# Spreading a bound over the partitions: a product with ones (sum) in place of a product with the identity and a maximum

## The chip, the cores and the metric

One core of a Trainium2 chip runs the whole program in one launch. The metric is device time in microseconds (us). The kernel before was run three times on its own: 1235.79, 1236.59 and 1240.24 us; the median is 1236.59 us.

## The reference

Three layers follow each other. An attention over 4 batches, 8 heads, 576 positions and head size 64 keeps only scores within tau of their row's maximum. Its output, 2304 tokens by 512, goes through two dense layers with a hidden size of 2048, each with its own elementwise function between two products.

```python
scores = scale * np.matmul(q, k.transpose(0, 1, 3, 2))
thresh = np.max(scores, axis=-1, keepdims=True) - tau
scores = np.where(scores >= thresh, scores, -1000000000.0)
attn = np.exp(scores - np.max(scores, axis=-1, keepdims=True))
attn = attn / (np.sum(attn, axis=-1, keepdims=True) + 1e-09)
x = np.matmul(attn, v)                      # heads side by side: 2304 x 512
...
h = x @ w_in                                # first layer ("moe1")
P = a[0] + a[1] * h + a[2] * h2 + a[3] * h3
Q = 1.0 + np.abs(b[0]) * np.abs(h) + np.abs(b[1]) * h2
x = (P / (Q + 1e-06)) @ w_out
...
h = x @ w_in                                # second layer ("moe2")
g = np.where(h >= 1, h, np.where(h <= -1, 0.0, (h + 1) ** 2 / 4.0))
out = g @ w_out
```

## The kernel before

**Two halves for every number.** TensorE multiplies in float16. Every operand is therefore scaled by a power of two and split into a high and a low half, and a product is three products of halves. The scale must come from a bound on the operand's size, and all 128 partitions must use the same one. So for each piece of input the kernel computes a number in each partition, brings these 128 numbers together in every partition, and then takes a power of two from the result (`root`: a shift and mask at L169, a multiply and maximum at L172, a reciprocal at L173). Bringing them together is the job of `everywhere` (L179): for each of n columns a float32 product of the column, repeated 128 times, with the identity matrix puts all 128 numbers side by side in every partition (L188), and VectorE takes their maximum (L189).

**Where it is called.** Each of the two layers has 8 chunks of weights with 2 halves each: x = 0 from w_in, x = 1 from w_out. `convert` (L233) loads a half (1 MB), turns it from wide words into float32 on VectorE (L229 to L231), lets TensorE build a product of it with itself (L254), reduces that on VectorE (L255) into `bound`, calls `everywhere` and `root`, and splits (`split`: ScalarE L218 and L209, GpSimd L213). `prep_pair` (L334) does the like for q and k of a pair of heads, with two columns (n = 2): squares summed on ScalarE (L345), `everywhere`, `root`, some small constants, then the split (L215, L216) and a transposing DMA of the halves (L365). `everywhere` is also called for v, for the norm of the first layer's weights and for each block of tokens between the two layers (L189 with place = acc).

**The order of work.** The first stage does batch 0's attention in a form of its own (`first_attention`), beside it all 16 halves of moe1's weights, and after that the 16 halves of moe2's weights (`stage_half`). Then come 8 phases, moe1 and moe2 for each batch; a phase is 24 steps: 3 blocks of 192 tokens by 8 chunks. A step is one `first_product` (24 matmuls, L863), the elementwise function on ScalarE, VectorE and GpSimd, and three steps later one `second_product` (24 matmuls, L877). When a chunk has been used for the last time in a phase its place is taken by the other layer's chunk, 1 MB from DRAM (`load_chunk`, L278). Attention of batch b + 1 runs beside the steps of batch b: for each of 4 pairs of heads 9 score rows, each with scores on TensorE (L396, L397), the clamp and row maximum on VectorE (L442), exponential on ScalarE (L403), mask on VectorE (L404), halves on ScalarE and GpSimd, a transposing DMA (L417) and the product with v (L430).

Every piece of code is given a priority by the step at which it is due (`at`), and a scheduler that estimates the engines' times puts all instructions in order on each engine ahead of the run. Each engine, and the DMA queue of SyncE (SP), then runs its list strictly in that order. Any instruction that is removed or gets another length can therefore move others, also far away.

Of the kernel before, what the change touches and what calls it, by code (L numbers as in the profile page):

```python
# [10 lines left out]
F32 = mybir.dt.float32  # L11
# [32 lines left out]
def tile_attention_moe_moe2(  # L44
# [18 lines left out]
    V, A, G, T, Q = nc.vector, nc.scalar, nc.gpsimd, nc.tensor, nc.sync  # L63
    B, H, S, D = q.shape
    P = 128
# [24 lines left out]
    ps_1 = ctx.enter_context(tc.tile_pool(name="ps_1", bufs=1, space=PSUM))  # L90
# [18 lines left out]
    def small(n, name, keep=False):  # L109
        if keep:  # L110
            return cp.tile([P, n], F32, name=name)
        tag = "".join(x for x in name if x.isalpha() or x == "_").rstrip("_")
        return sp.tile([P, n], F32, name=name, tag=f"s{n}_{tag}", bufs=4 if tag in ("mx", "nt") else 2)
# [51 lines left out]
    def root(name, f, src, up, even=False, n=1, keep=False):  # L165


        s = small(n, name + "_s", keep)
        V.tensor_scalar(f.bitcast(I32), src.bitcast(I32), 1, 0x3F000000 if even else 0x3F800000,  # L169
                        op0=ALU.logical_shift_right, op1=ALU.bitwise_and)  # L170
        top = TOP / 2 if even else TOP
        V.tensor_scalar(f, f, up / top, (2.0 if even else 1.0) * TINY / top, op0=ALU.mult, op1=ALU.max)  # L172
        V.reciprocal(s, f)  # L173
        return s
# [5 lines left out]
    def everywhere(name, src, n, keep=False, place=None):  # L180


        r = small(n, name, keep)
        if place is None:
            place = ps_1.tile([P, 512], F32, name="pm" + name, tag="aux")
        pm = place[:, 0 : n * P].rearrange("p (n q) -> p n q", n=n)
        for i in range(n):
            T.matmul(pm[:, i], src[:, i : i + 1].to_broadcast([P, P]), ident, start=True, stop=True)  # L188
        V.tensor_reduce(r, pm, axis=AX.X, op=ALU.max)  # L189
        return r  # L190

    wide = w1_in.dtype != F32
    words = 2 if wide else 1
    raw_type = I32 if wide else F32
# [5 lines left out]
    f_w = [[small(NCH, f"f_w{m}{x}", True) for x in range(2)] for m in range(2)]  # L202
# [3 lines left out]
    def split(hi, lo, src, scale=None, on_vector=True):  # L206

        if scale is None:
            A.copy(hi, src)  # L209

            n = E // 4 if tuple(src.shape) == (P, E) else None
            for p in [slice(c, c + n) for c in range(0, E, n)] if n else [slice(None)]:
                G.tensor_tensor(lo[:, p], src[:, p], hi[:, p], op=ALU.subtract)  # L213
        elif on_vector:
            A.activation(hi, src, AF.Copy, scale=scale)  # L215
            V.scalar_tensor_tensor(lo, src, scale, hi, op0=ALU.mult, op1=ALU.subtract)  # L216
        else:
            A.activation(src, src, AF.Copy, scale=scale)  # L218
            split(hi, lo, src)

    def as_float(raw, name):

        if not wide:
            return raw
        src = raw.rearrange("p (n w) -> p n w", w=2)
        t = mp.tile([P, E], I32, name="wt" + name, tag="wt", bufs=N_WT)
        V.tensor_scalar(t, src[:, :, 1], 0x07FFFFFF, 3, op0=ALU.bitwise_and, op1=ALU.logical_shift_left)  # L229
        V.scalar_tensor_tensor(t, src[:, :, 1], -0x40000000, t, op0=ALU.bitwise_and, op1=ALU.bitwise_or)  # L230
        V.scalar_tensor_tensor(t, src[:, :, 0], 29, t, op0=ALU.logical_shift_right, op1=ALU.bitwise_or)  # L231
        return t.bitcast(F32)

    def convert(m, i, x, dst, on_vector):

        if x == 0:
            raw = rp.tile([P, KT, CF * words], raw_type, name=f"rw{m}_{i}_0", tag="rw")
            src = w_in_dram[m][:, i * CF * words : (i + 1) * CF * words].rearrange("(kt p) f -> p kt f", p=P)
        else:
            raw = rp.tile([P, NF, DM * words], raw_type, name=f"rw{m}_{i}_1", tag="rw")  # L240
            src = w_out_dram[m][i * CF : (i + 1) * CF, :].rearrange("(f p) d -> p f d", p=P)
        (A if m == 0 and i == 0 else Q).dma_start(raw, src)
        name = f"{m}_{i}_{x}"
        src = as_float(raw.rearrange("p a b -> p (a b)"), name)
        hi, lo = dst[:, 0:E], dst[:, E : 2 * E]
        columns = m == 0 and x == 0
        bound = gram[:, i : i + 1] if columns else small(1, "mb" + name)
        pg = ps_1.tile([P, 512], F32, name="pg" + name, tag="aux")
        parts = NF if columns else 1
        top = src.bitcast(BF16).rearrange("p (n c f w) -> p n c f w", c=parts, f=P, w=2)[..., 1]  # L250
        n = top.shape[1]
        for c in range(parts):
            for k in range(n):
                T.matmul(pg[:, c * P : (c + 1) * P], top[:, k, c], top[:, k, c], start=(k == 0), stop=(k == n - 1))  # L254
        V.tensor_reduce(bound, pg[:, 0 : parts * P], axis=AX.X, op=ALU.max)  # L255
        s = root("pw" + name, f_w[m][x][:, i : i + 1], everywhere("mw" + name, bound, 1), 2.0**64, even=m == 1 and x == 1)
        split(hi, lo, src, s, on_vector)
        if i == NCH - 1 and (m, x) != (0, 0):
            f_max[m][x] = small(1, f"f_max{m}{x}", True)
            V.tensor_reduce(f_max[m][x], f_w[m][x], axis=AX.X, op=ALU.max)  # L260
# [26 lines left out]
    def whole(x):  # L287
        return x[..., 0 : NT * P, :].rearrange("h (p t) d -> p h (t d)", t=NT)
# [45 lines left out]
    def prep_pair(b, pr, on_vector=True):  # L334
        raws = rp.tile([P, 2, C + 1, D], F32, name=f"rqk{b}_{pr}", tag="rqk", bufs=1)
        raw = raws[:, :, 0:C, :]
        for x, src in enumerate((q, k)):
            Q.dma_start(raws[:, x].rearrange("p (a c) d -> p a (c d)", a=2)[:, :, 0 : NT * D],
                        whole(src[b, 2 * pr : 2 * pr + 2]))
            for ab in range(2):  # L340
                Q.dma_start(raw[ab * ST : (ab + 1) * ST, x, NT, :], src[b, 2 * pr + ab, NT * P :, :])
        mx = small(2, f"mqk{b}_{pr}")
        qk = ap.tile([P, 2, C, 2 * D], F16, name=f"qk{b}_{pr}", tag="qk", bufs=1)
        for x in range(2):
            A.activation(qk[:, x, :, 0:D], raw[:, x], AF.Square, scale=2.0**-32, accum_out=mx[:, x : x + 1])  # L345
        f = small(2, f"qkf{b}_{pr}")
        s = root(f"qkr{b}_{pr}", f, everywhere(f"mqke{b}_{pr}", mx, 2), 2.0**96, n=2)

        con = sp.tile([P, 4], F32, name=f"con{b}_{pr}", tag="con", bufs=3)
        V.scalar_tensor_tensor(con[:, 0:1], f[:, 0:1], cflag, f[:, 1:2], op0=ALU.mult, op1=ALU.mult)  # L350
        V.tensor_scalar(con[:, 1:2], con[:, 0:1], -1.0, None, op0=ALU.mult)
        V.scalar_tensor_tensor(con[:, 2:3], s[:, 0:1], tau8, s[:, 1:2], op0=ALU.mult, op1=ALU.mult)
        V.tensor_tensor(con[:, 2:3], con[:, 2:3], tlow, op=ALU.min)
        if b == 0:
            V.tensor_scalar(con[:, 3:4], con[:, 2:3], STEEP, -LARGEST, op0=ALU.mult, op1=ALU.max)
        for x in range(2):
            split(qk[:, x, :, 0:D], qk[:, x, :, D : 2 * D], raw[:, x], s[:, x : x + 1], on_vector)
        if b > 0 or pr < 2:
            qkT = ap.tile([P, 2 * C, P], F16, name=f"qkT{b}_{pr}", tag="qkT")
            qT, kT = qkT[:, 0:C], qkT[:, C : 2 * C]  # L360
            kT2 = ap.tile([P, C, P], F16, name=f"kT2{b}_{pr}", tag="kT2")
            if b == 0 and pr == 0:
                turned(qk, qT, kT, kT2)
                return con, qT, kT, kT2
            Q.dma_start_transpose(out=qkT, in_=qk.rearrange("p x c d -> p (x c d)"))  # L365
        else:
            qT, kT, kT2 = (ap.tile([P, C, P], F16, name=f"{x}{b}_{pr}", tag="eT" if pr == 2 else "hl", bufs=N_ROW)
                           for x in ("qT", "kT", "kT2"))
            for x, t in enumerate((qT, kT)):
                Q.dma_start_transpose(out=t, in_=qk[:, x].rearrange("p c d -> p (c d)"))  # L370
        Q.dma_start(kT2[0:D], kT[D : 2 * D])
        Q.dma_start(kT2[D : 2 * D], kT[0:D])
        return con, qT, kT, kT2
# [515 lines left out]
    for n in range(N_FIRST):  # L889
        with at(36 * n / N_FIRST - 40):  # L890
            next(att)
        while halves and len(halves) * N_FIRST > 2 * NCH * (N_FIRST - 1 - n):
            with at(2.4 * (2 * NCH - len(halves)) - 39.5):
                i, x = halves.pop(0)
# [83 lines left out]
```

## Time and profile before

| | |
|---|---|
| median of three runs | 1236.59 us (1235.79 to 1240.24) |
| the profiled execution's own time | 1239.17 us |
| its span | 1237.1 us |
| mean granted TensorE clock | 0.963 |
| busy: TensorE matmul, weight load | 1095.3 us (89%), 988.4 us (80%) |
| busy: VectorE, ScalarE, GpSimd | 979.3 (79%), 839.5 (68%), 542.7 us (44%) |
| chain that ended last | TensorE 40%, VectorE 24%, DMA 11%, GpSimd 9%, issue 9%, ScalarE 6% |

The shares are averages over stages of very different kinds. Up to about 275 us batch 0's attention and the conversion of the weights fill the time; from 275 us the 8 phases follow, at first with the next batch's attention beside them and from 1046 us without. Steps are counted here by their second product: step 0's starts near 275 us, step 8's near 318, step 24's near 396, step 32's near 429 and step 48's near 524.

### The profile page before, as it was taken

To read this page: it belongs to the slowest core of one execution; us is meant where nothing else is said; L and a number is where in the kernel's file an instruction comes from. 1 tells how busy PE (TensorE), PEld (TensorE's weight loads), DVE (VectorE), ACT (ScalarE), POOL (GpSimd) and SP (SyncE) were. 2 spreads that over 40 slices of the span, in tenths; PEclk is the share of its full clock that TensorE was granted. 3 is DMA by queue.
4 is the path that set the end of the run, shared out by engine and by line. 5 is a ranking of instruction groups with operands and counts; after the bars stand their busy time and mean duration, and the time that the engine had idled before them with its cause. 6 is when DMAs were issued, how large, how long until landed. Compare 5 with 4: busy or idle time off the path is not lost.

```text
span 1237.1 us, 31750 instructions
## 1 busy us (share of the span) xinstructions
PE 1095.3 (89%) x12636; PEld 988.4 (80%) x12636; DVE 979.3 (79%) x2362; ACT 839.5 (68%) x1532; POOL 542.7 (44%) x698
## 2 busy tenths in 40 slices
PE   2778788588899999898888998998899999999998
PEld 1445456477888989898778888997888998999997
DVE  8887896999997377799997766899996768896431
ACT  2577777698887377677875766887675667775332
POOL 2445545656666266322564454223563553222221
PEclk9888888899899999999999999999999999999999
DMA  7677576635269158813785639422984467007000
GB/s 220 224 205 252 210 266 238 220 93 137 49 151 249 29 111 185 218 28 90 183 225 95 115 64 250 136 50 68 242 195 71 81 171 221 15 2 261 15 14 27
DMA packets 217845, 175.51 MB, mean 142 GB/s; under 512 B 179680, under 2 KB 190944, under 8 KB 209504
## 3 DMA queue, kind: packets, MB, share of 16 engines
q1 hardware_dynamic: 216464, 171.38, 52.6%
q8 instruction: 99, 1.62, 0.5%
q10 hardware_dynamic: 1232, 2.10, 0.5%
q14 instruction: 50, 0.41, 0.1%
HBM read 106.83 MB, written 21.50 MB: 104 GB/s over the span
## 4 chain that ended last, share of the span: by engine, by line
PE 40%; DVE 24%; DMA 11%; POOL 9%; issue 9%; ACT 6%; SPq 1%; DVEq 0%; ACTq 0%; POOLq 0%
PE acc L877 15%; PE ph L863 15%; DMA eT<-hl 8%; POOL hl L415 3%; PE pv L613 2%; PE pv L430 2%; DVE t L746 2%; POOL wh L213 2%; DVE e L404 2%; DVE t L751 2%; DVE sc L442 2%; POOL gg L213 1%; DVE t L757 1%; DVE t L748 1%; DVE t L747 1%
## 5 line engine op out<-in xcount | busy, mean ns | idle before, releaser
L877 PE MATMUL acc<-gg,wc 128*128 128x192 f16 x4608 | 427.6, 247 | 10.9 <-DVE mye L189 4.9
L863 PEld LDWEIGHTS <-wc 128*128 128x128 f16 x4608 | 388.9, 99 | 24.4 <-issue 16.5
L877 PEld LDWEIGHTS <-wc 128*128 128x128 f16 x4608 | 384.1, 98 | 12.6 <-issue 11.2
L213 POOL TENSOR_TENSOR gg<-t,gg 128x384 f16<-128x384 f32 x192 | 192.9, 1006 | 380.1 <-ACT gg L209 308.0
L863 PE MATMUL ph<-xT,wc 128*128 128x192 f16 x2304 | 218.1, 252 | 13.3 <-DVE t L748 13.2
L863 PE MATMUL ph<-yT,wc 128*128 128x192 f16 x2304 | 213.4, 246 | 3.7 <-DVE t L748 2.5
L415 POOL TENSOR_TENSOR hl<-e,hl 128x256 f16<-128x256 f32 x216 | 160.6, 764 | 0.0
L209 ACT CAST gg<-t 128x384 f16<-128x384 f32 x192 | 96.9, 508 | 75.1 <-DVE t L810 36.8
L809 DVE SCALAR_TENSOR_TENSOR t<-t,c 128x384 f32<-128x384 f32 x96 | 66.2, 690 | 88.9 <-ACT t L808 87.0
L404 DVE SCALAR_TENSOR_TENSOR e<-sc,nt,e 128x576 f32<-128x576 f32 x108 | 97.5, 903 | 28.1 <-ACT e L403 27.9
L413 POOL TENSOR_TENSOR hl<-e,hl 128x64 f16<-128x64 f32 x108 | 42.3, 391 | 147.7 <-ACT hl L412 134.0
L403 ACT ACTIVATE e<-sc,nt,con 128x576 f32<-128x576 f32 x108 | 93.3, 864 | 4.6 <-POOL hl L415 0.2
L808 ACT ACTIVATE t<-ph,c 128x384 f32<-128x384 f32 x96 | 63.9, 667 | 45.6 <-PE ph L863 45.3
L430 PE MATMUL pv<-v,eT 128*128 128x65 f16 (+3 forms) x1680 | 71.4, 195 | 25.2 <-DMA eT<-hl 24.1
L442 DVE TENSOR_SCALAR_CACHE_REDUCE sc<-s 128x576 f32<-128x576 f32 x108 | 80.8, 748 | 15.2 <-PE s L397 14.5
L412 ACT CAST hl<-e 128x576 f16<-128x576 f32 x108 | 72.1, 667 | 28.6 <-DVE e L404 28.0
L430 PEld LDWEIGHTS <-eT 128*128 128x128 f16 (+1 forms) x1680 | 64.0, 101 | 33.9 <-DMA eT<-hl 30.0
L744 ACT ACTIVATE t<-ph,sc 128x384 f32<-128x384 f32 x96 | 55.3, 576 | 50.6 <-PE ph L863 50.4
L213 POOL TENSOR_TENSOR wc<-wt,wc 128x256 f16<-128x256 f32 x64 | 55.1, 894 | 63.8 <-ACT wc L209 63.8
L749 ACT ACTIVATE t<-t,lc 128x384 f32<-128x384 f32 x96 | 67.8, 708 | 15.3 <-DVE t L746 14.9
L213 POOL TENSOR_TENSOR wh<-wt,wh 128x256 f16<-128x256 f32 x64 | 58.9, 950 | 35.8 <-ACT wh L209 35.7
L751 DVE SCALAR_TENSOR_TENSOR t<-t,ka,t 128x384 f32<-128x384 f32 x96 | 67.7, 705 | 8.7 <-ACT t L750 8.3
(238 smaller groups left out, 1910.9 us busy)
## 6 DMA issues: line engine op xcount, KB each, us to landing
wc<-scratch SPq DMA_DIRECT2D x56, 1024.0 KB, 5.9
rw<-in_moe_w_in_dram SPq DMA_DIRECT2D x15, 1024.0 KB, 5.7
rw<-in_moe_w_out_dram SPq DMA_DIRECT2D x15, 1024.0 KB, 5.4
scratch<-wc SPq DMA_DIRECT2D x8, 1024.0 KB, 4.5
scratch<-wh SPq DMA_DIRECT2D x16, 512.0 KB, 3.7
rqk<-in_q_dram SPq DMA_DIRECT2D x16, 256.0 KB, 3.1
rqk<-in_k_dram SPq DMA_DIRECT2D x16, 256.0 KB, 3.1
kT<-qkT SPq DMA_DIRECT2D x26, 144.0 KB, 2.5
```

The lines of the kernel that those rows point to most:

```text
L209: A.copy(hi, src)
L213: G.tensor_tensor(lo[:, p], src[:, p], hi[:, p], op=ALU.subtract)
L403: A.activation(e, s, AF.Exp, bias=nb, scale=con[:, 0:1])
L404: V.scalar_tensor_tensor(e, s, th, e, op0=ALU.is_ge, op1=ALU.mult)
L412: A.copy(hi, e)
L415: G.tensor_tensor(lo_w[:, p], e[:, whole][:, p], hi[:, whole][:, p], op=ALU.subtract)
L430: T.matmul(pv[rows, 0:w], eT[:, c, cols], vv[:, h * NT + x if x < NT else H * NT + h, at : at + w], start=(n == 0), stop=(n == len(blocks) ...
L442: V.tensor_scalar(s, banks[:, 0:S], 1.0, -LARGEST, op0=ALU.mult, op1=ALU.max, accum_out=mx)
L749: A.activation(r, u, AF.Ln, bias=lc[:, 1:2], scale=lc[:, 0:1])
L751: V.scalar_tensor_tensor(s, s, ka[:, 0:1], r, op0=ALU.add, op1=ALU.mult)
L863: last = T.matmul(ph[:, f, :], w[:, wx, kt, f * P : (f + 1) * P], rhs, start=(n == 0), stop=(n == 3 * KT - 1))
L877: T.matmul(dst, w[:, wx, f, d * P : (d + 1) * P], gg[:, gx, f, :], start=(i == 0 and f == 0 and n == 0 and d % 2 == 0), stop=(i == NCH - 1 ...
```

## The change

A new vector `one` holds 1.0 in every partition, and a new function `total` multiplies a 128 by 128 matrix of ones with the n columns themselves, one float32 product with n columns. Its result is the sum over the partitions instead of the maximum, and it stands in every partition already, so no reduction follows: `root` reads the PSUM tile. `convert` uses `total` for all halves but moe2's w_in (m = 1, x = 0): 24 of 32. `prep_pair` uses it for all 16 pairs. The other callers of `everywhere` stay. Bounds become larger where sums replace maxima; the powers of two follow from them, and nothing else in the code is edited.

```diff
+    one = small(1, "one", True)
+    G.memset(one, 1.0)
+
+    def total(name, src, n):
+
+        pm = ps_1.tile([P, 512], F32, name="ps" + name, tag="aux")[:, 0:n]
+        T.matmul(pm, one.to_broadcast([P, P]), src, start=True, stop=True)
+        return pm
...
-        s = root("pw" + name, f_w[m][x][:, i : i + 1], everywhere("mw" + name, bound, 1), 2.0**64, even=m == 1 and x == 1)
+        s = root("pw" + name, f_w[m][x][:, i : i + 1], (everywhere if m == 1 and x == 0 else total)("mw" + name, bound, 1), 2.0**64, even=m == 1 and x == 1)
...
-        s = root(f"qkr{b}_{pr}", f, everywhere(f"mqke{b}_{pr}", mx, 2), 2.0**96, n=2)
+        s = root(f"qkr{b}_{pr}", f, total(f"mqke{b}_{pr}", mx, 2), 2.0**96, n=2)
```

Lines below the new function are 9 higher in the changed kernel (L255 becomes L264, L278 becomes L287, L417 becomes L426, L442 becomes L451, L748 becomes L757).

**One weight half on VectorE, in the first stage.** The kernel before, around the half of chunk 5 from moe1's w_out (mb: its bound; pmmw: the 128 numbers in PSUM; mw: their maximum; f_w, pw: the two results of `root`; mx: batch 0's row maxima):

```order
L255 TENSOR_REDUCE mb_5_1_1395<-pg_5_1_1396 128x1
L544 TENSOR_REDUCE mx_2_985<-sm_11_1066 128x1
L189 TENSOR_REDUCE mw_5_1_1406<-pmmw_5_1_1407 128x1
L169 TENSOR_SCALAR f_w_136<-mw_5_1_1406 128x1
L172 TENSOR_SCALAR f_w_136<-f_w_136 128x1
L544 TENSOR_REDUCE mx_2_985<-sm_12_1085 128x1
L173 RECIPROCAL pw_5_1_s<-f_w_136 128x1
```

The changed kernel at the same place:

```order
L264 TENSOR_REDUCE mb_5_1_1363<-pg_5_1_1364 128x1
L240 SCALAR_TENSOR_TENSOR wt_6_0_1507<-rw_6_0_1505,wt_6_0_1507 128x1024
L173 RECIPROCAL pw_5_0_s<-f_w_137 128x1
L553 TENSOR_REDUCE mx_2_959<-sm_03_987 128x1
L169 TENSOR_SCALAR f_w_138<-psmw_5_1_1374 128x1
L172 TENSOR_SCALAR f_w_138<-f_w_138 128x1
```

The reduction of L189 is gone, L169 reads the PSUM tile psmw, and the order of the neighbours is another.

**SP's queue at the change from moe1 to moe2 of batch 0.** The kernel before, from the first load of a moe2 chunk (wc) on (eT: transposes of batch 1's rows, the first number the pair of heads; qkT_2: transposed q and k of pair 2; rqk: input of pair 3):

```order
L278 DMA wc_0_3774<-scratch_134 128x4096
L417 DMA_TRANSPOSE eT_1_0_1_5094<-hl_1_0_1_5089 128x9x128
L278 DMA wc_1_3872<-scratch_134 128x4096
L365 DMA_TRANSPOSE qkT_2_4665<-qk_2_4643 128x18x128
L278 DMA wc_2_3939<-scratch_134 128x4096
L417 DMA_TRANSPOSE eT_1_0_2_5138<-hl_1_0_2_5133 128x9x128
L278 DMA wc_3_4044<-scratch_134 128x4096
L371 DMA kT_2_4666<-qkT_2_4665 64x1152
L372 DMA kT_2_4666<-qkT_2_4665 64x1152
L417 DMA_TRANSPOSE eT_1_1_0_5307<-hl_1_1_0_5302 128x9x128
L278 DMA wc_4_4111<-scratch_134 128x4096
L417 DMA_TRANSPOSE eT_1_1_1_5353<-hl_1_1_1_5348 128x9x128
```

The changed kernel, from the same load on:

```order
L287 DMA wc_0_3713<-scratch_136 128x4096
L287 DMA wc_1_3811<-scratch_136 128x4096
L287 DMA wc_2_3878<-scratch_136 128x4096
L426 DMA_TRANSPOSE eT_0_2_1_4770<-hl_0_2_1_4765 128x9x128
L287 DMA wc_3_3980<-scratch_136 128x4096
L287 DMA wc_4_4047<-scratch_136 128x4096
...
L287 DMA wc_7_4512<-scratch_136 128x4096
L374 DMA_TRANSPOSE qkT_2_4598<-qk_2_4579 128x18x128
L380 DMA kT_2_4599<-qkT_2_4598 64x1152
L381 DMA kT_2_4599<-qkT_2_4598 64x1152
L426 DMA_TRANSPOSE eT_0_2_2_4818<-hl_0_2_2_4813 128x9x128
L426 DMA_TRANSPOSE eT_1_0_0_4991<-hl_1_0_0_4986 128x9x128
```

In the kernel before the transposes of pair 1's rows stand between the loads; in the changed kernel the last row of pair 0 and all rows of pair 1 stand behind the eighth load, and only one transpose stands among the loads.

**VectorE in the same place.** The kernel before, third block of tokens of moe1 (t_0_2_1: its second step; sc, e: batch 1's rows):

```order
L442 TENSOR_SCALAR sc_1_0_0_5046,mx_1_0_0_5044<-s_1_0_0_5039 128x576
L746 SCALAR_TENSOR_TENSOR t_0_2_1_3481<-t_0_2_1_3481,qc 128x384
L463 RECIPROCAL rd_0_2_4494<-rd_0_2_4494 128x2
L747 TENSOR_TENSOR t_0_2_1_3482<-t_0_2_1_3482,ph_0_2_1_3456 128x384
L444 TENSOR_SCALAR nt_1_0_0_5045<-mx_1_0_0_5044,con_1_3965 128x1
L465 TENSOR_TENSOR xs_0_2_4497<-pv_0_2_4444,rd_0_2_4494 128x128
L751 SCALAR_TENSOR_TENSOR t_0_2_0_3384<-t_0_2_0_3384,ka_1935,t_0_2_0_3383 128x384
```

The changed kernel, the same step:

```order
L755 SCALAR_TENSOR_TENSOR t_0_2_1_3425<-t_0_2_1_3425,qc 128x384
L766 SCALAR_TENSOR_TENSOR t_0_2_0_3329<-t_0_2_0_3329,t_0_2_0_3330 128x384
L756 TENSOR_TENSOR t_0_2_1_3426<-t_0_2_1_3426,ph_0_2_1_3400 128x384
L757 SCALAR_TENSOR_TENSOR t_0_2_1_3426<-t_0_2_1_3426,ka_1893,ph_0_2_1_3400 128x384
L760 SCALAR_TENSOR_TENSOR t_0_2_1_3426<-t_0_2_1_3426,ka_1893,t_0_2_1_3425 128x384
L755 SCALAR_TENSOR_TENSOR t_0_2_2_3525<-t_0_2_2_3525,qc 128x384
```

Batch 1's rows are no longer between the steps here. In the changed kernel three rows of batch 1 stand in the order between the second products of step 8 and step 24, and the pairs' rows are level again with the kernel before at step 33.

## Rows read from the trace of the kernel before

**Rows 1.** Busy time by stretch: start:end, us, each engine, clock, DMA, GB/s

```profile
0.00:275.00 275.00, 200.01 (x1350) 138.47 (x1351) 233.02 (x518) 189.76 (x301) 137.47 (x164) 0.88 0.66 217
318.00:396.00 78.00, 69.16 (x840) 64.19 (x838) 71.49 (x171) 60.78 (x119) 50.92 (x63) 0.96 0.68 170
396.00:434.00 38.00, 38.00 (x506) 37.69 (x504) 16.91 (x54) 15.16 (x29) 10.26 (x12) 1.00 0.15 34
434.00:512.00 78.00, 73.05 (x963) 66.78 (x960) 59.98 (x154) 56.57 (x110) 44.85 (x66) 0.98 0.75 157
524.00:672.00 148.00, 132.93 (x1641) 126.14 (x1639) 138.08 (x351) 110.25 (x211) 60.16 (x74) 0.99 0.56 131
788.00:919.00 131.00, 118.80 (x1441) 111.76 (x1439) 125.37 (x316) 99.63 (x191) 50.76 (x64) 0.99 0.51 123
1046.00:1237.00 191.00, 184.57 (x2214) 183.32 (x2211) 109.97 (x232) 96.37 (x171) 40.53 (x45) 0.99 0.16 57
```

**Rows 2.** Costliest groups, shapes apart: the instructions that the change touches

```profile
L188 PE MATMUL pmmqke<-ident,mqk 128*128 128x128 f32 x64 | 13.0, 318 | 14.9 <-ACT lc L151 7.8 <-ACT qk L345 7.1
L188 PE MATMUL pmmw<-ident,mb 128*128 128x128 f32 x48 | 12.8, 355 | 9.6 <-DVE mb L255 9.4
L189 DVE TENSOR_REDUCE mw<-pmmw 128x1 f32<-128x128 f32 x32 | 9.1, 283 | 6.0 <-PE pmmw L188 6.0
L189 DVE TENSOR_REDUCE mqke<-pmmqke 128x2 f32<-128x256 f32 x16 | 6.6, 414 | 3.6 <-PE pmmqke L188 3.6
```

**Rows 3.** Single instructions: ns min/median/max, first and last start in us

```profile
L189 DVE TENSOR_REDUCE mw<-pmmw x32: 276/282/293, 20.2 to 264.5; 128x1 f32<-128x128 f32 x32
L169 DVE TENSOR_SCALAR f_w<-mw x32: 131/144/154, 21.5 to 265.2; 128x1 int32<-128x1 int32 x32
L169 DVE TENSOR_SCALAR qkf<-mqke x16: 152/167/875, 18.3 to 938.2; 128x2 int32<-128x2 int32 x16
L462 DVE TENSOR_SCALAR rd<-pv x60: 138/150/160, 305.1 to 1041.7; 128x2 f32<-128x2 f32 x48, 128x1 f32<-128x1 f32 x12
```

**Rows 4.** L189 on VectorE up to 275 us: busy us and count

```profile
0.00:275.00 275.00, 11.98 (x40) 0.88 0.66 217
```

**Rows 5.** Timeline of one pair's call in batch 3's attention: start, us

```profile
936.98 0.53 PEld L188 LDWEIGHTS pmmqke<-ident,mqk 128*128 128x128 f32 x4
937.06 0.64 PE L188 MATMUL pmmqke<-ident,mqk 128*128 128x128 f32 x4
937.73 0.42 DVE L189 TENSOR_REDUCE mqke<-pmmqke 128x2 f32<-128x256 f32 x1 [0.65 <-PE pmmqke L188]
```

**Rows 6.** L442 (one pair of instructions per attention row): busy us and count

```profile
318.00:396.00 78.00, 7.69 (x22) 0.96 0.68 170
396.00:434.00 38.00, 0.76 (x2) 1.00 0.15 34
434.00:512.00 78.00, 13.61 (x36) 0.98 0.75 157
```

**Rows 7.** The chain that ended last, 376 to 402 us: start, us, what

```profile
376.50 8.56 DMA eT<-hl
385.07 8.14 DMA rqk<-in_k_dram
395.64 4.12 PE acc L877 x48
399.76 1.98 PE ph L863 x24
```

**Rows 8.** SP's queue: first and last of the eight chunk loads

```profile
355.53 0.36 SPq L278 DMA_DIRECT2D wc<-scratch  x1
389.28 0.53 SPq L278 DMA_DIRECT2D wc<-scratch  x1
```

**Rows 9.** Who waited for whom, TensorE, whole span: us, times, longest us

```profile
PE pv L430 <- DMA eT<-hl: 24.1, 27, 2.2
```

**Rows 10.** The page: chain that ended last, share of the span by engine

```profile
PE 40%; DVE 24%; DMA 11%; POOL 9%; issue 9%; ACT 6%; SPq 1%; DVEq 0%; ACTq 0%; POOLq 0%
```

## Prediction

> **What bounds the kernel now.** I read the busy time by stretch first [rows 1], because the change touches three kinds of stretch and its worth differs in each. From 1046 us on nothing is edited: TensorE is busy 184.6 of 191 us there, and that part stays. Up to 275 us no engine is full, but VectorE is nearest to it: 233.0 of 275 us, 85%, against 200.0 for TensorE and 189.8 for ScalarE. Where attention runs beside moe1 steps VectorE is the fullest engine: 71.5 of 78 us from 318 to 396, 138.1 of 148 from 524 to 672, 125.4 of 131 from 788 to 919, which is 92 to 96%. From 396 to 434 us there is nearly no attention, TensorE is busy for all 38 us and VectorE for 16.9. So work taken from VectorE counts in the first three kinds of stretch and not in the last. The second view is the costliest groups [rows 2], for the price of what goes; the third is the chain of waits around 380 us [rows 7], for what the new order does.
>
> **The change part by part.**
>
> *Reductions removed.* 24 of the 32 reductions for weight halves go, at 283 ns, and all 16 for pairs, at 414 ns [rows 2]. That is 24 x 0.283 = 6.8 us and 16 x 0.414 = 6.6 us, 13.4 us of VectorE. The halves all lie before 264.5 us [rows 3]. Of the 40 instructions of L189 before 275 us [rows 4] 32 are for halves; two for v and one for the norm leave 5 for pairs. So the first stage loses 6.8 + 5 x 0.414 = 8.9 us of VectorE, and the time after it 11 x 0.414 = 4.6 us.
>
> In the first stage VectorE has 42 us of idle time, mostly waits for others, so not all of the 8.9 us shortens the path. The ends are 0 (all becomes waiting) and 8.9. Nothing there is full enough to hold the path alone, and a reduction of 0.28 us stands in a chain that crosses TensorE, VectorE and ScalarE once per half; I take half, 4.5 us.
>
> After 275 us, about 8 of the 11 pairs lie in stretches where VectorE is 92 to 96% busy. There 0.41 us less is close to 0.41 us: 8 x 0.41 = 3.3 us. The other three lie beside a full TensorE. I take 3.0 us, ends 0 and 4.6.
>
> *L169 reads PSUM.* The row for a small instruction of the same kind that reads PSUM is L462, median 150 ns; L169 from SBUF takes 144 ns with one column and 167 with two [rows 3]. So I cost the move at nothing; the ends are 40 times -17 ns and +6 ns, under 1 us either way. [...]
>
> *TensorE.* A pair's call is four weight loads and four matmuls with 128 columns, 0.64 us on TensorE [rows 5]. The order of the changed kernel has one float32 matmul with two columns in their place, which by the pattern of the others is two loads and two matmuls. Half of 0.64 is 0.32 us less per pair. A half's call keeps both of its loads; its matmuls have 1 column instead of 128. No row shows a float32 matmul of 1 column, so its price lies between nothing and the 355 ns of the 128 columns [rows 2]; I take it that the load sets the pace and nothing is won. The pairs' 0.32 us lies in the same places as the reduction, mostly beside VectorE's work, and I don't count it again; beside a full TensorE it is what makes the other three pairs worth something (3 x 0.32 = 1 us, the upper end of the 3.0 above).
>
> The wait that TensorE has for the bound of a half, L188 on L255, 9.4 us [rows 2], stays: the new matmul needs the same number from the same reduction.
>
> *The new order.* This is the largest unknown. In the kernel before 11 rows of batch 1's attention run from 318 to 396 us (22 instructions, two a row) and one from 396 to 434 [rows 6]. In the changed order only 3 stand between the second products of step 8 and step 24, so 8 rows move from the first stretch, where VectorE is 92% busy and TensorE idles for 8.8 us, to the steps 24 to 33, where TensorE had no gap and VectorE was busy for 16.9 of 38 us. What a row costs TensorE I get from 434 to 512 us: 13 steps at 2 x 1.98 us [rows 7] are 51.5 us, TensorE was busy 73.05 [rows 1], and 18 rows ran there [rows 6], so 1.2 us a row. The first stretch then has 69.2 - 9.6 = 59.6 us of TensorE work; dense it would take 60 us, with all of its present idle time 68.4. I take 66, 12 less than 78. The second takes 9.6 us more. Net 2.4 us less; the ends are 8.8 less (all idle time goes) and, if the rows' own chain holds up the later steps, more than before (the last rival).
>
> *The loads.* In the kernel before the transposes stand between eight 1 MB loads from 355.5 to 389.3 us [rows 8], and the chain that ended last goes through one that took 8.56 us and a load that took 8.14 us beside them [rows 7]. With one transpose among the loads this knot goes. I count nothing for it beyond the 2.4 us, since it is the same idle time.
>
> *Sum.* 4.5 + 3.0 + 2.4 = 9.9 us less. The profiled execution took 1239.17 us (span 1237.1 and 2.1 us around it), 2.6 us above the median of the runs. Its time less the sum is 1229.3, the median less the sum 1226.7; I predict the middle, 1228 us.
>
> **The rivals.**
>
> *The saved time was not on the path.* VectorE's 8.9 us in the first stage become waits for the weights' DMA, GpSimd or ScalarE, and the order after it changes nothing. For it: VectorE already idles 15% there, and the chain of the whole span is VectorE's for only 24% [rows 10]. Against it: 92 to 96% in three later stretches. Then only about 3 us are won: 1233 to 1237 us.
>
> *All of it is on the path.* 8.9 + 4.6 + 8.8 = 22.3 us less, 1214 to 1217 us. Against it: it needs every gap of the first stage to close.
>
> *The rows come too late (slower).* In the changed order 9 rows of pair 1 stand between steps 24 and 33, and each must run through TensorE, VectorE, ScalarE, GpSimd and a transpose before its product with v, which stands in TensorE's own strict order in front of moe2's matmuls. Waits of that kind already cost 24.1 us in 27 times, at most 2.2 us each [rows 9]. If each of 11 rows that moved (those of pair 1 and the last two of pair 0) waits 2.2 us, that is 24 us; against the 7.5 us of direct savings it decides from 0.7 us a row on, and with 1.2 us a row the change is 13.2 - 7.5 = 6 us slower, about 1243 us. For it: the same knot of order and strict queues exists already. Against it: VectorE, ScalarE and GpSimd are less than half busy in that stretch [rows 1], so a row gets through sooner than before.
>
> **How the numbers follow.** A change below 0.5%, 6.2 us, can't be told from none here. The forecast, with everything between 1217 and 1230.4 us, gets 0.54, of which the full saving has 0.04; the saving off the path 0.32; the late rows 0.14, of which a little ends within 0.5%. So faster 0.54, same 0.34, slower 0.12. The range runs from the full saving's upper end, 1217, to 1241, where most of the slower case is still in: outside are about 0.05 below and 0.13 above. The likeliest case alone spans 1220 to 1231.
>
> **What would show it.** L189 should count 25 in place of 65 instructions, L169 should stay near 150 ns, and TensorE's new matmul should take a call to about half for pairs. Step 0's second product should start 4 to 5 us before 275 us; step 33's another 3 us earlier still; VectorE in the stretches of batches 2 and 3 about 1.7 us less busy each, and the stretches as much shorter. TensorE should have hardly a gap between steps 8 and 24. The forecast is wrong if step 0 starts where it did, or if TensorE waits more than 24 us in all for transposes, with the new waits in steps 24 to 38.

## The result and the profile after

The changed kernel takes 1250.1 us (median of 15 runs) where the kernel before takes 1237.0 (15 runs beside it): ratio 1.0098, 95% interval 1.0076 to 1.012. It is slower by 1%, or 12 us by the ratio, where 0.7% faster was forecast. Its profiled execution took 1248.73 us with a span of 1246.9, at a mean granted TensorE clock of 0.949 (0.963 before).

Busy time by stretch of the changed kernel, the stretches cut at the starts of the same steps as in [rows 1] where those were right (24, 33, 48). Columns: us, then busy us (and instructions) of TensorE's matmuls, its weight loads, VectorE, ScalarE, GpSimd; granted clock, DMA share, GB/s.

```profile
0.00:275.00 275.00, 185.96 (x1199) 126.68 (x1200) 226.70 (x490) 185.85 (x295) 145.31 (x164) 0.84 0.70 222
318.00:389.00 71.00, 67.55 (x827) 65.63 (x825) 62.98 (x145) 52.65 (x100) 39.40 (x40) 1.00 0.44 134
389.00:443.00 54.00, 45.56 (x591) 42.33 (x589) 31.39 (x91) 31.24 (x61) 23.70 (x38) 0.94 0.47 82
443.00:534.00 91.00, 82.39 (x1143) 75.92 (x1141) 67.00 (x176) 65.34 (x126) 42.79 (x70) 1.00 0.76 168
1056.00:1247.00 191.00, 184.46 (x2212) 183.20 (x2210) 109.92 (x232) 96.32 (x171) 40.59 (x45) 1.00 0.16 56
```

VectorE is relieved: over the whole span it is busy for 970.4 us against 979.3. In the first 275 us TensorE is busy 14 us less than before as well (186.0 against 200.0 us): by then the changed kernel has got less far. From step 24 to step 33, 389 to 443 us, TensorE stands still for 8.4 of 54 us where it was busy for all of 38. Behind step 33 the stretches are as long as before (91 and 191 us against 90 and 191).

What was edited, by line and tile: out<-in, partitions x elements, count, then busy us and mean ns of one, and the idle time ahead. L200 is the product with ones.

```profile
L200 PE MATMUL psmw<-mb,one 128*128 128x1 f32 x32 | 5.9, 254 | 1.7 <-DVE mb L264 1.7
L200 PE MATMUL psmqke<-mqk,one 128*128 128x2 f32 x32 | 5.6, 246 | 12.0 <-ACT qk L354 12.0
L189 DVE TENSOR_REDUCE mw<-pmmw 128x1 f32<-128x128 f32 x8 | 2.3, 286 | 1.5 <-PE pmmw L188 1.5
```

And L169, the first reader of a bound, one instruction at a time (ns min/median/max): from PSUM in the first two rows, from SBUF in the third.

```profile
L169 DVE TENSOR_SCALAR f_w<-psmw x24: 145/150/160, 19.0 to 254.5; 128x1 int32<-128x1 int32 x24
L169 DVE TENSOR_SCALAR qkf<-psmqke x16: 145/152/160, 15.2 to 950.2; 128x2 int32<-128x2 int32 x16
L169 DVE TENSOR_SCALAR f_w<-mw x8: 140/154/157, 147.0 to 243.8; 128x1 int32<-128x1 int32 x8
```

So each edited instruction costs what it was priced at or less. TensorE's waits over the whole span (us, times, longest) are where the two kernels part; the first row answers [rows 9], 24.1 us before:

```profile
PE pv L439 <- DMA eT<-hl: 41.9, 28, 8.0
...
PE s L405 <- DVE sc L451: 10.6, 8, 6.5
```

The second row is TensorE waiting for VectorE to read a score row out of PSUM. In the kernel before it was:

```profile
PE s L396 <- DVE sc L442: 7.2, 11, 1.3
```

The chain that ended last answers [rows 10]: VectorE's share fell from 24 to 15%, and the time did not.

```profile
PE 38%; DVE 15%; DMA 10%; issue 9%; POOL 7%; ACT 7%; SPq 1%; DVEq 0%; POOLq 0%; ACTq 0%
```

A correction to the text ahead of the prediction: the early step times given there are too late. In the kernel before the second product of step 0 starts at 244 us, not 275, and that of step 8 at 305, not 318; steps 24 to 48 are right. So [rows 1] starts its second stretch 13 us behind step 8; from step 8 on it is:

```profile
305.00:396.00 91.00, 82.16 (x1013) 76.94 (x1010) 84.22 (x198) 73.78 (x147) 61.29 (x74) 0.96 0.63 153
```

Starts of second products, in us, counted in the traces of the profiled executions (the other columns are the experiments below). Each column is one execution, up to 3 us off its kernel's median:

| step | before | after | sum, old order | maximum, new order | three repairs | three repairs, 128 columns |
|---|---|---|---|---|---|---|
| 0 | 244 | 259 | 247 | 256 | 255 | 256 |
| 8 | 305 | 317 | 306 | 315 | 315 | 315 |
| 24 | 396 | 389 | 394 | 387 | 386 | 387 |
| 33 | 434 | 443 | 433 | 440 | 432 | 433 |
| 48 | 524 | 534 | 522 | 531 | 526 | 522 |
| 144 | 1046 | 1056 | 1044 | 1052 | 1050 | 1040 |
| 188 | 1222 | 1232 | 1220 | 1229 | 1227 | 1217 |

The changed kernel is 15 us late at step 0, 12 late at step 8, 7 us early at step 24, 9 late at step 33, and about 10 from there on. From step 8 to step 33 it is 3 us faster than the kernel before (126 us against 129).

### The profile page after: what moved, and what is told of

Its sections match the earlier page's. It is cut to its first block, busy times and chain, and to the rows that moved or that the text cites. A ratio compares the mean times of both kernels' runs of the same rounds, so it can differ in the third digit from the quotient of the medians.

```text
span 1246.9 us, 31660 instructions
## 1 busy us (share of the span) xinstructions
PE 1092.0 (88%) x12604; PEld 987.6 (79%) x12604; DVE 970.4 (78%) x2322; ACT 842.7 (68%) x1532; POOL 549.2 (44%) x699
## 3 DMA queue, kind: packets, MB, share of 16 engines
q10 hardware_dynamic: 1232, 2.10, 0.5%
## 4 chain that ended last, share of the span: by engine, by line
PE 38%; DVE 15%; DMA 10%; issue 9%; POOL 7%; ACT 7%; SPq 1%; DVEq 0%; POOLq 0%; ACTq 0%
PE ph L872 16%; PE acc L886 16%; DMA eT<-hl 6%; POOL hl L424 3%; PE pv L439 2%; DMA qkT<-qk 2%; POOL wh L222 2%; DVE e L413 2%; POOL gg L222 1%; DVE t L760 1%; DVE t L755 1%; DVE t L766 1%; DVE t L756 1%; PE s L405 1%; ACT hl L421 1%
## 5 line engine op out<-in xcount | busy, mean ns | idle before, releaser
L222 POOL TENSOR_TENSOR gg<-t,gg 128x384 f16<-128x384 f32 x192 | 190.0, 991 | 389.1 <-ACT gg L218 310.6
L872 PE MATMUL ph<-xT,wc 128*128 128x192 f16 x2304 | 221.8, 255 | 16.2 <-DVE t L757 7.8
L872 PE MATMUL ph<-yT,wc 128*128 128x192 f16 x2304 | 218.9, 248 | 2.0 <-DVE t L757 2.0
L439 PE MATMUL pv<-v,eT 128*128 128x65 f16 (+3 forms) x1680 | 71.6, 197 | 42.1 <-DMA eT<-hl 41.9
L451 DVE TENSOR_SCALAR_CACHE_REDUCE sc<-s 128x576 f32<-128x576 f32 x108 | 80.8, 749 | 9.6 <-PE s L406 9.0
L222 POOL TENSOR_TENSOR wc<-wt,wc 128x256 f16<-128x256 f32 x64 | 60.7, 980 | 58.2 <-ACT wc L218 58.2
L222 POOL TENSOR_TENSOR wh<-wt,wh 128x256 f16<-128x256 f32 x64 | 63.4, 1019 | 43.9 <-ACT wh L218 43.9
```

The source lines that it names most:

```text
L439: T.matmul(pv[rows, 0:w], eT[:, c, cols], vv[:, h * NT + x if x < NT else H * NT + h, at : at + w], start=(n == 0), stop=(n == len(blocks) ...
L451: V.tensor_scalar(s, banks[:, 0:S], 1.0, -LARGEST, op0=ALU.mult, op1=ALU.max, accum_out=mx)
L872: last = T.matmul(ph[:, f, :], w[:, wx, kt, f * P : (f + 1) * P], rhs, start=(n == 0), stop=(n == 3 * KT - 1))
```

## Experiments

My theory: the new order of the queues is what costs, not the sum. Its first rival: the sum itself (product with ones, PSUM read) costs. Its second: the order of the kernel before is a good draw and any edit loses it. For most of the experiments the order of each engine's queue is written out as a table of positions and chained with issue-order edges (`NoSync`: order without a semaphore). In the traces the sum in the old order and the maximum in the new order run every engine's and SP's sequence of the other kernel, apart from the instructions exchanged.

```diff
+def keep_order(tc):
...
+        for d in steps:
+            at += d
+            x = rows[engine][at]
+            if last is not None:
+                tc.add_manual_dep(x, last.name, mybir.DependencyInfo(mybir.DependencyClass.NoSync, mybir.DependencyReason.DATA), reason="order")
+            last = x
...
     while pending:
         with at(st + 1.5):
             finish_step()
+    keep_order(tc)
```

**Order against sum.** Sum in the old order:

> The changed kernel's instructions, every engine's queue put in the order of the kernel before (the 16 second products and 40 reductions that the change removes are left out of it, the memset of the ones is put in). If the loss is the new order of the queues: 1223 to 1238 us, 12 to 27 below the changed kernel, not above the kernel before. If the sum itself (the product with ones, the read of PSUM) costs: 1245 to 1255, as the changed kernel.

1238.77 us, ratio 1.0026 (1.0009 to 1.0044).

Maximum in the new order:

> The kernel before with its identity products and maxima, every engine's queue put in the order of the changed kernel (the removed instructions stand where their readers stand). If the loss is the order: 1245 to 1262 us, as the changed kernel or up to 9 more, for the 8.9 us of VectorE that it still has. If the sum itself costs: 1232 to 1240, as the kernel before.

1244.56 us, ratio 1.0075 (1.0047 to 1.0103).

Neither theory takes all. The order alone costs 0.75%, the sum alone 0.26%, and together they are the 0.98% of the change. The first run is just above its range and the second just below: 13.4 us less of VectorE in the old order gave nothing. TensorE's two long waits are there with the maximum in the new order (us, times, longest, from 246 to 434 us), where no sum is:

```profile
PE s L517 <- DVE sc L563: 8.0, 2, 6.8
PE pv L551 <- DMA eT<-hl: 6.4, 3, 5.6
```

With the sum in the old order no such wait in that stretch is longer than 1.2 us.

One row for each of four kernels shows that the end of the first stage follows the order and hardly the sum: the last operation of the division on each of batch 0's four pairs (ns min/median/max, first and last start). Before, then sum in the old order:

```profile
L629 DVE SCALAR_TENSOR_TENSOR x<-x,d x4: 747/1164/1220, 90.1 to 227.2; 128x576 f32<-128x576 f32 x4
```

```profile
L761 DVE SCALAR_TENSOR_TENSOR x<-x,d x4: 750/1166/1221, 91.9 to 229.8; 128x576 f32<-128x576 f32 x4
```

Maximum in the new order, then the changed kernel:

```profile
L750 DVE SCALAR_TENSOR_TENSOR x<-x,d x4: 1109/1220/1447, 91.6 to 234.1; 128x576 f32<-128x576 f32 x4
```

```profile
L638 DVE SCALAR_TENSOR_TENSOR x<-x,d x4: 1107/1221/1718, 90.2 to 234.0; 128x576 f32<-128x576 f32 x4
```

The last pair starts this at 227 to 230 us in the old order and at 234 in the new, with a sum or a maximum.

**Where in the order.** New order up to step 0, old behind:

> The changed kernel's instructions; its own order up to the second product of step 0, the order of the kernel before for all that is left. If the place that costs is the first stage (step 0 15 us late): 1245 to 1255 us. If it is the transpose of 8 us at 394 us, behind pair 2's on SP: 1230 to 1240. If the sum itself costs: 1245 to 1255.

1243.84 us, 1.0067 (1.004 to 1.0094).

Old order up to step 0, new behind:

> The changed kernel's instructions; the order of the kernel before up to the second product of step 0, its own order for all that is left. If the place that costs is the first stage: 1225 to 1240 us. If it is the late transpose at 394 us: 1245 to 1255. If the sum itself costs: 1245 to 1255.

1247.41 us, 1.0107 (1.0075 to 1.0139).

The first lies outside its ranges: it loses 0.4% more than the sum in the old order, so the new order costs something in the first stage. The second has the whole loss of the changed kernel with the old order in the first stage. That need not lie far behind the cut: its step 0 starts at 262 us, 15 later than in the sum in the old order, after two waits of TensorE for VectorE at the joint of the two orders (3.9 and 3.1 us, ending at 252 and 258 us). So neither run places the loss cleanly.

The order of the changed kernel with the old one from step 24 on:

> The changed kernel's instructions; its own order up to the second product of step 24, the order of the kernel before for all behind. It keeps what the new order does up to 390 us (TensorE's wait of 6.5 us at 267 us for the first row of batch 1, step 0 15 us later) and loses the late transpose at 394 us. If the late transpose is the greater part: 1240 to 1245 us. If what stands ahead of step 0 is: 1246 to 1252.

1257.35 us, 1.0172 (1.0135 to 1.0209), outside both ranges. The joint itself costs: steps 22 to 24 take 36 us (375 to 411) where the changed kernel takes 12, and nine score rows run there against one; rows that the new order puts behind step 24 and the old one ahead of it all stand at the joint. It says nothing on the question.

**The place near step 24.** The changed kernel, from the timeline (start, us, engine, and in brackets the idle time before and what ended it): SP's queue, ScalarE, TensorE.

```profile
385.95 6.86 SPq L374 DMA_TRANSPOSE qkT<-qk  x1
397.25 0.48 SPq L380 DMA_DIRECT2D kT<-qkT  x1
397.79 0.59 SPq L381 DMA_DIRECT2D kT<-qkT  x1
398.48 1.42 SPq L426 DMA_TRANSPOSE eT<-hl  x1
...
388.48 0.67 ACT L817 ACTIVATE t<-ph,c 128x384 f32<-128x384 f32 x1 [0.18 <-PE ph L872]
397.26 0.68 ACT L354 ACTIVATE qk<-rqk 128x576 f16<-128x576 f32 x1 [8.11 <-DMA qkT<-qk]
...
402.02 1.54 PE L439 MATMUL pv<-v,eT 128*64 128x65 f16 x28 [7.96 <-DMA eT<-hl]
```

Pair 2's transpose holds SP's queue until 392.8 us (by the profile it waits 6.9 us for a score product of TensorE), and its landing holds the copies of k behind it until 397; the transpose that TensorE waits for (row eT_0_2_2) stands behind all of them. On ScalarE the squares of pair 3, which overwrite the buffer that this transpose reads, stand ahead of everything else for 8.1 us. In the old order that row's transpose stands five places ahead of pair 2's. First, the transpose alone:

```diff
 SP
+transpose eT_0_2_2 <- hl_0_2_2
 transpose qkT_2 <- qk_2
 copy kT_2 <- qkT_2 (twice)
-transpose eT_0_2_2 <- hl_0_2_2
```

> The changed kernel in its own order with one instruction of SP's queue moved: the transpose of row eT_0_2_2 stands before the transpose of pair 2's q and k and the two copies of its k, no longer behind them. If TensorE's wait of 8.0 us at 394 us is lost time that nothing gives back: 1241 to 1244 us, 6 to 9 below the changed kernel. If the lost time is elsewhere, or the wait only changes its name: 1247 to 1252.

1248.57 us, 1.0083 (1.0043 to 1.0123): the wait only changed its name, that is, TensorE now waits for another instruction. ScalarE and TensorE in this run:

```profile
396.38 0.68 ACT L474 ACTIVATE qk<-rqk 128x576 f16<-128x576 f32 x1 [8.15 <-DMA qkT<-qk]
...
401.33 0.59 PE L525 MATMUL s<-qkT 128*128 128x512 f16 x1 [7.26 <-DVE sc L571]
```

ScalarE stands as long as before, and TensorE now stops 7.3 us one row on. So I moved the squares as well; their reader on TensorE comes some 30 us later (at 441.9 us in the changed kernel, the new place being near 410), so nothing waits for them.

```diff
 ScalarE (with the move on SP)
-square qk_3 <- rqk_3 (twice)
 round yT_2 <- y_2
 ... (12 more)
 round hl_1_0_1 <- e_1_0_1
+square qk_3 <- rqk_3 (twice)
```

> The changed kernel in its own order with two moves: on SP the transpose of eT_0_2_2 ahead of pair 2's transpose (as before), and on ScalarE the two squares of pair 3, which wait for pair 2's transpose to land, from ahead of y's rounding to behind the rounding of row hl_1_0_1, still ahead of their reader. If what stops TensorE for 7 to 8 us near step 24 is ScalarE's queue standing behind these squares: no wait over 3 us between 385 and 420 us, and 1241 to 1245 us. If that time is given back to other waits: 1247 to 1251.

1242.88 us, 1.0069 (1.0044 to 1.0093), as expected. All that TensorE waited for between 385 and 420 us:

```profile
PE pv L559 <- DMA eT<-hl: 1.4, 1, 1.4
```

Two moves of three instructions give back 0.3 of the 1%. The interval still overlaps that of the changed kernel; the run with all repairs below is the test.

**The place at 267 us.** The changed kernel: VectorE rounds v and computes constants while TensorE waits for it to take batch 1's first score row out of PSUM (L451).

```profile
267.11 2.11 DVE L225 SCALAR_TENSOR_TENSOR v<-rv,v_s,v 128x512 f16<-128x512 f32 x2
...
273.04 0.75 DVE L451 TENSOR_SCALAR_CACHE_REDUCE sc<-s 128x576 f32<-128x576 f32 x1
...
273.84 0.59 PE L405 MATMUL s<-qkT 128*128 128x512 f16 x1 [6.48 <-DVE sc L451]
```

```diff
 VectorE
+read sc_0_0_0, nt_0_0_0
 round v (two pieces)
 constant k8
+read sc_0_0_1
 ... (polynomial, v, constants)
-read sc_0_0_0, nt_0_0_0
 ...
-read sc_0_0_1
```

> The changed kernel in its own order, with two score rows of batch 1 (sc_0_0_0 and sc_0_0_1) moved 8 to 11 places forward on VectorE's queue, ahead of the rounding of v and of constants that nothing waits for yet. If TensorE's wait of 6.5 us at 267 us is lost time: the wait under 3 us and 1243 to 1247 us. If it is given back later, as step 24 is reached earlier than in the old order anyway: 1248 to 1252.

1245.78 us, 1.0067 (1.0039 to 1.0094): lost time too, again with overlapping intervals. TensorE's wait there is:

```profile
PE s L525 <- DVE sc L571: 3.2, 2, 2.4
```

**SP in the first stage.** In the new order some loads of raw halves stand behind stores that wait for GpSimd (32.5 us in 13 waits ahead of 280 us, the longest 5.5).

```diff
 SP (first of several such places up to batch 1's first transpose)
+load rw_2_0
 store scratch <- wh_0_0
-load rw_2_0
```

> The changed kernel in its own order, but SP's queue up to the transpose of batch 1's first pair stands as before: the loads of the second layer's raw halves ahead of the stores of finished ones. If these loads are what makes batch 0's last pair 6 us late (234 us, 228 in the old order): pair done by 230 us, step 0's second product by 253, and 1244 to 1247 us. If something else does: pair at 233 to 235 and 1248 to 1252.

1250.94 us, 1.0104 (1.0074 to 1.0134): my reason falls. The last pair comes later still, by 10 us, which neither forecast had:

```profile
L758 DVE SCALAR_TENSOR_TENSOR x<-x,d x4: 1107/1220/1716, 95.8 to 244.4; 128x576 f32<-128x576 f32 x4
```

**Together.** All four moves, then without SP's first stage:

> The changed kernel in its own order with the moves of the two runs before and the two moves near step 24 all together. If these places are all that the new order costs and add up: 1235 to 1240 us, as the sum in the old order (1.001 to 1.004 of the kernel before). If the repairs are given back to other waits: 1241 to 1246.

1245.89 us, 1.0062 (1.0035 to 1.0089), in the range of repairs that are given back; it carries the harm of the loads (last pair at 243 us).

> The changed kernel in its own order with the two moves near step 24 and VectorE's two score rows earlier; SP's first stage as the changed kernel has it. If the two places add up (1.0098 less 0.0029 less 0.0031 of the kernel before): 1239 to 1242 us. If one repair is given back to the other: 1243 to 1246.

1240.43 us, 1.0029 (1.0002 to 1.0056): the two places add up, and here the interval is clear of the changed kernel's. What was done in one and the same stretch, from 246 to 434 us, by the kernel before, the changed kernel and the three repairs:

```profile
246.00:434.00 188.00, 167.92 (x2019) 158.89 (x2019) 157.87 (x394) 140.83 (x270) 108.32 (x126) 0.95 0.49 120
```

```profile
246.00:434.00 188.00, 160.55 (x1893) 151.14 (x1893) 155.58 (x373) 140.49 (x269) 100.98 (x114) 0.92 0.43 106
```

```profile
246.00:434.00 188.00, 167.75 (x2025) 157.63 (x2025) 162.78 (x393) 147.79 (x283) 107.59 (x124) 0.95 0.45 111
```

In the changed kernel TensorE gets through 1893 matmuls there where the kernel before does 2019; with the repairs it does 2025. The sum of its waits for transposes says less: with the repairs it is still 38.6 us over the span, but the longest is 3.8 and no longer 8.0.

**The narrow product.** What is left, 0.3%, is as much as the sum cost in the old order. The kernels with a sum had lower clocks (mean 0.961 for the sum in the old order, against 0.967 for the kernel before in the runs beside it, and 0.953 for the changed kernel), so I gave TensorE its old work back: 128 equal columns for each bound, in as many calls as the identity product, in otherwise the same order.

```diff
-    pm = ps_1.tile(...)[:, 0:n]
-    T.matmul(pm, one.to_broadcast([P, P]), src, start=True, stop=True)
-    return pm
+    pm = ps_1.tile(...)[:, 0 : n * P].rearrange("p (n q) -> p n q", n=n)
+    for i in range(n):
+        T.matmul(pm[:, i], one.to_broadcast([P, P]), src[:, i : i + 1].to_broadcast([P, P]), start=True, stop=True)
+    return pm[:, :, 0]
```

Old order, new order, four repairs, three repairs:

> As the sum in the old order (1238.8 us, 1.0026 of the kernel before, at a mean clock of 0.961 against 0.967), but the product with the ones moves 128 columns for each bound, all alike, in as many calls as the identity product did: TensorE does the work of before, VectorE still does without its 40 maxima. If the 3 us of the sum come from TensorE being less busy and so granted a lower clock: 1230 to 1236, clock 0.966. If from the read of PSUM or the rounding of the sum: 1238 to 1241, clock 0.961. If they are chance: 1231 to 1238.

> The changed kernel in its own order, its product with the ones moving 128 columns for each bound in as many calls as the identity product, so that TensorE has the work of before. If the narrow product lowers the granted clock (0.953 in the changed kernel): clock 0.959 to 0.963 and 1243 to 1247 us. If not: clock 0.953 and 1248 to 1252.

> As the four repairs, with the product with ones 128 columns wide. If the narrow product costs 3 to 6 us through TensorE's clock: 3 to 6 us below the four repairs on the same chip, at a clock higher by 0.004 or more. If the difference seen so far is chance: within 2 us of it.

> As the three repairs, with the product with ones 128 columns wide. From the three pairs so far, the wide product has a mean clock higher by 0.006 to 0.008 and is 0.05 to 0.3% faster. If that is the narrow product's own cost: a clock higher by 0.005 or more and 1 to 4 us below the three repairs. If it is chance: within 1 us on either side.

| order | narrow: ratio, mean clock | 128 columns: us, ratio (interval), mean clock |
|---|---|---|
| old | 1.0026, 0.961 | 1238.4, 1.0011 (0.999 to 1.0032), 0.968 |
| new | 1.0098, 0.953 | 1242.5, 1.0068 (1.0044 to 1.0093), 0.961 |
| four repairs | 1.0062, 0.955 | 1243.5, 1.0057 (1.0035 to 1.0078), 0.961 |
| three repairs | 1.0029, 0.957 | 1235.5, 0.9999 (0.9976 to 1.0023), 0.961 |

Only the last two lines compare runs of one chip. No single line settles the time, as the intervals overlap, but all four go the same way: 0.15, 0.30, 0.05 and 0.30%, mean 0.20%, 2.5 us, with a clock higher by 0.004 to 0.008. Weighted by their intervals the four give 0.19%, plus or minus 0.16 (an estimate). The clocks came about as forecast, the times less so: 1238.4 us in the old order is outside the 1230 to 1236 that went with the higher clock, four repairs gave 2.3 us where 3 to 6 or under 2 were forecast, three repairs 4.9 us where it was 1 to 4.

In the traces' clock records the granted share of TensorE's clock is 1 or 0.5. Behind step 33 it is 0.5 for 18.5, 27.7, 28.6 and 22.6 us with the narrow product, in the order of the table, and for 12.6, 13.1, 15.7 and 17.8 us with the wide one. But the kernel with halves only, below, has 27.6 us there, and all its narrow products lie ahead of step 33; so this does not settle the cause. The products of the three repairs, narrow and then wide:

```profile
L320 PE MATMUL psmw<-mb,one 128*128 128x1 f32 x32 | 6.0, 257 | 2.0 <-DVE mb L384 2.0
...
L320 PE MATMUL psmqke<-mqk,one 128*128 128x2 f32 x32 | 5.6, 246 | 12.0 <-ACT qk L474 12.0
L320 PE MATMUL psmw<-gram,one 128*128 128x1 f32 x16 | 2.9, 254 | 3.0 <-DVE gram L384 2.9
```

```profile
L321 PE MATMUL psmqke<-mqk,one 128*128 128x128 f32 x64 | 12.3, 314 | 10.6 <-ACT lc L271 7.8 <-ACT qk L475 2.7
...
L321 PE MATMUL psmw<-mb,one 128*128 128x128 f32 x32 | 7.6, 322 | 1.4 <-DVE mb L385 1.4
L321 PE MATMUL psmw<-gram,one 128*128 128x128 f32 x16 | 3.9, 333 | 3.0 <-DVE gram L385 2.9
```

**One part alone, and no part.** Halves only:

> Only the bounds of the weight halves are sums; pairs of q and k keep the identity product and the maximum. The order is the scheduler's own for this program. If each small edit only draws another order: anywhere from 1230 to 1255 us, and the waits of the changed kernel at 267 and 394 us come or go with the order. If the halves' sum does it by itself: 1247 to 1252.

1249.11 us, 1.0101 (1.0065 to 1.0137), inside both ranges.

Pairs only:

> Only the pairs of q and k use the sum; weight halves keep the identity product and the maximum. The order is the scheduler's own. If each edit draws another order and the kernel before has a good one: 1238 to 1255 us. If the halves' sum does the harm: 1234 to 1240.

1239.03 us, 1.0021 (0.9998 to 1.0044).

The kernel before, redrawn:

```diff
-WEIGHTS = (0, 20)
+WEIGHTS = (0.5, 20.5)
```

> The kernel before, not one instruction added, removed or replaced; only the due times of the second layer's weight halves are half a step later (the two numbers 0, 20 are 0.5, 20.5), which draws another order. If the time hangs on the order and the order of the kernel before is a good one among many: 1240 to 1255 us. If the order is worth little: 1233 to 1239.

1237.16 us, 1.0018 (0.9997 to 1.0039), in the range for an order that is worth little. So not every redraw costs 1%; the second rival falls as far as one redraw can show. Of the four orders that the scheduler drew here for a small edit, two lose 1% (the change, halves only) and two 0.2% (pairs only, this one). Pairs alone fit both of their ranges. They wait as long for transposes as the change does, 43.9 us in all and 6.7 at the longest, so that sum does not tell a slow order from another. Halves alone lose as much as the whole change, but not at its places: in its profile step 33 starts at 436 us, 2 later than before, and step 128 at 972 (957 before). It drew an order of its own, and where that loses I did not follow up.

## Why the prediction was wrong

- **The new order** is the step that failed. It was priced at -2.4 us, from TensorE's work in two stretches between step 8 and step 33, and at nothing ahead of them; the maximum in the new order measures +0.75%, 9 us. Ahead of step 8 the changed kernel is already 15 us late (step 0), the maximum in the new order 12. Between step 8 and step 33 the moves came as said: steps 8 to 24 became dense and shorter (91 to 72 us), steps 24 to 33 longer (38 to 54). Their net of -3 us is near the -2.4 by luck: the first stretch became 19 us shorter where 12 were forecast, and the second 16 us longer where I had counted 9.6 us of work and no wait; TensorE stands still in it for 8.4 us. The pieces of the two stops were at hand in the changed order: a transpose behind another pair's on SP, squares that wait for that pair ahead of ScalarE's other work, score rows behind v's rounding on VectorE. Moving six instructions at these two places gives back 0.69% of the 0.98%; step 0 stays 11 us late, and the steps up to 33 make up for it.
- **The removed reductions.** 25 of L189 remain, as said. The forecast put 4.5 of 8.9 us of the first stage and 3.0 of 4.6 us behind it on the path. In the old order with TensorE's work unchanged the ratio is 1.0011 (0.999 to 1.0032): at most 0.1% of the 0.6% came. Batch 0's last pair ends no earlier, and the rival "not on the path" had this term right. "Half" was a guess between ends, and 85% busy did not make VectorE the bound here. Behind the first stage the 92 to 96% did not either: in the sum in the old order steps 48 to 96 and 96 to 144 take 263 and 259 us, 263 and 258 in the kernel before.
- **L169 from PSUM** is right at nothing: 150 and 152 ns, against 154 from SBUF in the same run.
- **TensorE.** A pair's call came to about half, as said (0.31 us at 949.9 us, against 0.64 in [rows 5]). "Nothing won" for a half is right in the rows only in part (a matmul takes 254 ns against 355 in [rows 2]), and the sum had no term for a loss. The narrow product costs about 0.2% by four pairs of kernels.
- **The rival "the rows come too late"** was given 0.14 and about 1243 us. Its sign is right and its place in part: waits for transposes grew from 24.1 to 41.9 us, with the longest near step 24. Its mechanism is not: no eleven rows at 2.2 us each, but one stop of 8.0 us that two queues of other engines make, another at 267 us, and the late step 0, both ahead of the place I looked at.
- **The tests.** Both signs of a wrong forecast came. Step 0 was to start 4 to 5 us earlier and started 15 later; the waits for transposes were to stay under 24 us and are 41.9, though the pairs alone show that this sum can be as large in a kernel 0.2% slower. TensorE between steps 8 and 24 has hardly a gap, as said (67.6 of 71 us busy).
- The last version, three repairs with 128 columns, equals the kernel before within its interval (0.9976 to 1.0023): 0.69% came back with two places of the order, 0.30% with the wide product. The saving on VectorE appears nowhere in it, and no version tried beats the kernel before.

Open: why the new order's first stage ends 6 us later and its step 0 starts 12 to 15 us late, since moving SP's loads made it worse; and through what the narrow product costs its 0.2%. The clock goes with it in all four pairs, but that the clock is the cause is argued, not shown.

## What to carry to other kernels

Where a scheduler draws the order, a small edit is two changes: price the new queues at the places where they differ, instruction by instruction on each engine and on SP, before pricing the instruction saved. Put the old order under the new instructions and the new order under the old ones to tell the two apart. An engine's wait that is repaired alone may move one row on (TensorE's 8.0 us came back as 7.3 here): follow it to the queue where it starts. Test a repair by the time, not by the sum of waits.

## What was not expected of the hardware

With three repairs a float32 matmul of one column takes 257 ns on average, one of 128 columns 322 ns: 128 times the columns cost a quarter more. With 9 us more of such work on TensorE (matmuls 23.8 against 14.5 us) the mean granted clock was higher (0.961 against 0.957 over 12 runs each, on one chip), and the kernel was not slower for it but 0.3% faster, with overlapping intervals.
